# Attention and two MoE layers on one core: 64-column value products, rotated keys in the last score step, and weight units spread over six slots

## Chip, core and metric

The kernel runs on one core of a Trainium2 chip. The metric is the device time of one execution in microseconds. Five engines work side by side, each through its own list of instructions in order: TensorE (PE, with its weight loads listed as PEld), VectorE (DVE), ScalarE (ACT), GpSimd (POOL) and SyncE (SP), which here issues the DMAs.

## What is computed

Attention with a position bias, and then two mixture-of-experts layers of one expert each, over 2304 tokens (4 batches of 576) with 8 heads of 64:

```python
scores = scale * np.matmul(q, k.transpose(0, 1, 3, 2))      # q, k, v: (4, 8, 576, 64)
x = (psi_rel / psi_i)[..., None]                            # from the positions alone
bias = np.maximum(x @ w1 + b1, 0.0) @ w2                    # 32 hidden, 8 heads
scores = scores + bias.transpose(2, 0, 1)[None]
attn = np.exp(scores - np.max(scores, axis=-1, keepdims=True))
attn = attn / (np.sum(attn, axis=-1, keepdims=True) + 1e-09)
x = np.matmul(attn, v)                                      # to (2304, 512)
h = x @ w_in                                                # 512 -> 2048
x = (h * np.clip(h + 3.0, 0.0, 6.0) / 6.0) @ w_out          # 2048 -> 512
gate = 1.0 / (1.0 + np.exp(-(x @ w_gate)))                  # 512 -> 1536
out = (gate * (x @ w_val)) @ w_out2                         # 1536 -> 512
```

## The kernel before

**Stages.** From 0 to 57 us the bias tables are made and written to DRAM (L572 on DVE, L557 on ACT, L578 on PE). From 57 to 341 us stands the attention, and from 341 to 1158 us the two MoE layers.

**Attention.** There are 16 passes (`n`, four pairs of heads by four batches). A pass has nine steps. Steps 0 to 7 take a block of 128 queries of one of the two heads against all 576 keys. Step 8 takes the 64 queries that are left of both heads, the first head's in partitions 0 to 63 and the second's in 64 to 127. One step is: scores on PE (L342, two halves of 288 keys, each from a high and a low part of K), bias added and the minimum taken on DVE (`u`, L346), exponential on ACT (L362), transposes of the probabilities on PE (L400 for 512 of the keys, 128 at a time, evacuated to `ptm` by DVE in L392 or ACT in L390). The 64 keys that are left, the last 64 for the first head and the first 64 for the second, are transposed for both heads in one (L415, `trans_rem`, into `ptr`). In step 8 the two heads lie in the two halves of the partitions of `Pm`, and their 512 keys start at different columns, so there are eight transposes of 64x64 (L408) with two evacuations, and for the rest two transposes (L418, L419) from a tile that has 64 columns of zeros in front.

**Attention times values.** Per half of the queries (`a`), `av` takes four pairs of products with 64 columns of weights, one per head, which go to the two halves of a PSUM bank's partitions (L432), and then one product of 128 weight columns for the rest of the keys of both heads (L435). The matrix unit takes an f32 operand in two passes, so the trace has two records for each such instruction.

**Softmax sums.** `invert` adds 1e-9 to the sums (L368), takes the reciprocal (L369), and ACT spreads them; PE transposes them (L379), and L444 multiplies the product by them.

**Weights for the MoE.** A weight unit is 512 KB. `Loader` takes it in by a DMA on SP (L159) and makes two f32r halves of it: ACT takes the magnitude (L175); DVE does a maximum (L176), a shift (L184) and two merges of raw and shifted words (L186, L188); ACT rounds it (L192) and POOL subtracts (L193). Ten units are prepared during the attention (`NPRE`), each written as one piece (`whole`) every sixth slot (`EVERY`); a slot is two steps. Two more are started by `PRIME` in the last slots.

**What sets the order.** The Tile framework's scheduler puts each instruction into its engine's list by the priority with which the code was written; `tc.issue_after` holds the loader behind the last load of V. In the same stretch POOL makes the low parts of Q and K for the next pass (`prep`, L314 and L318).

## Time and profile before

| | us |
|---|---|
| median of three runs (lowest, highest) | 1158.08 (1157.95, 1161.23) |
| the profiled execution, its span | 1160.52, 1158.7 |
| PE, DVE, ACT, POOL busy | 1135.9, 772.8, 588.4, 422.6 |
| bias tables, 0 to 57: PE, DVE, ACT, POOL busy | 45.51, 50.70, 50.09, 3.32 |
| attention, 57 to 341: the same | 280.78, 222.22, 226.12, 132.22 |
| MoE, 341 to 1158: the same | 809.64, 499.83, 312.20, 287.07 |

The profiled execution is 2.44 us above the median; its granted clock was 0.998 over the span. A busy share is an average over a stage, so the windows have to be read beside it. In a timeline, a row stands for a run of equal instructions; the last one's end is modelled and overlaps the next row, so what a run costs is taken from its start to the start of the next row.

### The profile page before, as it was taken

Reading aid. Unit: us, or ns where it says so; the run is one execution under the profiler, and the core shown is the slowest. Engines: PE = TensorE matmul, PEld = TensorE weight load, DVE = VectorE, ACT = ScalarE, POOL = GpSimd, SP = SyncE. Lnnn points to the kernel's source line nnn. Section 1 sums busy time; section 2 is a strip of 40 time slices with the busy share of each in tenths; the row PEclk is TensorE's granted clock in tenths of the full one; section 3 lists DMA queues with packets and bytes.
Section 4 is the critical chain, followed back from the end, with each engine's and each line's share of the span. In section 5 each row is a group of like instructions: output and inputs, shape, how many; then the busy total and the mean of one; then the engine's idle time right before and its main releaser. Section 6 shows DMA issues by size and latency. Waiting matters only on the chain.

```text
span 1158.7 us, 19146 instructions
## 1 busy us (share of the span) xinstructions
PE 1135.9 (98%) x6862; PEld 1012.2 (87%) x6862; DVE 772.8 (67%) x1495; ACT 588.4 (51%) x1296; POOL 422.6 (36%) x342
## 2 busy tenths in 40 slices
PE   8799999999999999999999999999999999999998
PEld 3277777777779999999999999999899898998997
DVE  8977878788868887355386775585367655644443
ACT  7988887877855545454455454342333222221221
POOL 0154544544316433232347445261333223311211
PEclk9999999999999999999999999999999999999999
DMA  6854436353213665249467759976878848757532
GB/s 203 298 162 110 158 95 183 112 165 103 78 55 110 209 218 200 101 174 340 167 228 255 253 189 357 395 261 251 308 254 309 311 165 299 285 181 258 191 109 73
DMA packets 83183, 236.82 MB, mean 204 GB/s; under 512 B 9616, under 2 KB 12304, under 8 KB 83088
## 3 DMA queue, kind: packets, MB, share of 16 engines
q1 hardware_dynamic: 83088, 235.60, 58.6%
q8 instruction: 54, 0.88, 0.3%
q14 instruction: 41, 0.34, 0.1%
HBM read 154.15 MB, written 81.41 MB: 203 GB/s over the span
## 4 chain that ended last, share of the span: by engine, by line
PE 84%; DVE 6%; ACT 2%; DMA 2%; issue 1%; POOL 1%; SPq 0%; POOLq 0%; DVEq 0%; ACTq 0%
PE o L673 17%; PE h L807 10%; PE o L807 10%; PE s L342 6%; PE o L862 6%; PE h L862 5%; PE h L611 5%; PE h L610 5%; PE h L612 5%; PE av L432 5%; PE tr L400 4%; PE av L435 1%; DVE z L186 1%; DVE u L346 1%; PE tr L379 1%
## 5 line engine op out<-in xcount | busy, mean ns | idle before, releaser
L673 PE MATMUL o<-gh,slot 128*128 128x384 f32 x768 | 196.0, 336 | 1.8 <-DVE take L392 1.8
L673 PEld LDWEIGHTS o<-gh,slot 128*128 128x128 f32 x768 | 139.2, 188 | 2.3 <-DVE take L392 2.1
L673 PE MATMUL o<-gl,slot 128*128 128x384 f32 x384 | 129.1, 336 | 0.7 <-DVE gl L659 0.7
L362 ACT ACTIVATE p<-u,stat 128x576 f32<-128x576 f32 x128 | 98.7, 773 | 29.2 <-DVE stat L346 28.4
L342 PE MATMUL s<-k,q 128*128 128x288 f32 x640 | 111.0, 309 | 0.7 <-ACT ptm L557 0.4
L346 DVE CUSTOM_DVE_ANT_0 u<-s,bias 128x576 f32<-128x576 f32 x128 | 93.6, 753 | 24.4 <-PE s L342 23.2
L843 POOL TENSOR_TENSOR gp<-s,gp 128x384 fp32r<-128x384 f32 x36 | 39.4, 1107 | 177.0 <-ACT gp L842 92.6
L617 DVE SCALAR_TENSOR_TENSOR g<-g,h 128x384 f32<-128x384 f32 x94 | 51.6, 549 | 70.2 <-ACT g L616 70.1
L659 DVE TENSOR_TENSOR gl<-g,gh 128x384 fp32r<-128x384 f32 x94 | 63.1, 671 | 48.3 <-ACT gh L658 45.8
L658 ACT CAST gh<-g 128x384 fp32r<-128x384 f32 x94 | 48.3, 513 | 91.6 <-DVE g L617 91.3
L193 POOL TENSOR_TENSOR hl<-corners,hl 128x512 fp32r<-128x512 f32 x42 | 57.2, 1366 | 94.3 <-ACT hl L192 79.3
L342 PEld LDWEIGHTS s<-k,q 128*128 128x128 f32 x640 | 88.8, 189 | 2.3 <-ACT ptm L557 0.6
L616 ACT ACTIVATE g<-h,half 128x384 f32<-128x384 f32 x94 | 54.3, 578 | 58.4 <-PE h L612 57.9
L807 PE MATMUL o<-x,slot 128*128 128x384 f32 x432 | 78.4, 336 | 1.4 <-DVE sum L787 1.4
L432 PE MATMUL av<-ptm,vn 128*64 128x288 f32 x512 | 77.8, 419 | 0.7 <-DVE x L444 0.7
L807 PE MATMUL h<-x,slot 128*128 128x384 f32 x432 | 77.8, 335 | 0.0
L807 PEld LDWEIGHTS o<-x,slot 128*128 128x128 f32 x432 | 75.1, 188 | 2.0 <-DVE sum L787 1.7
L807 PEld LDWEIGHTS h<-x,slot 128*128 128x128 f32 x432 | 75.2, 188 | 0.7
L400 PE MATMUL tr<-ident,p 128*128 128x128 f32 x512 | 72.2, 275 | 2.2 <-ACT inv L390 1.5
L673 PEld LDWEIGHTS o<-gl,slot 128*128 128x128 f32 x384 | 72.5, 189 | 1.3 <-DVE gl L659 1.3
L314 POOL TENSOR_TENSOR k<-early,one 128x576 fp32r<-128x576 f32 x30 | 34.4, 1167 | 106.3 <-DVE x L572 53.1
L843 POOL TENSOR_TENSOR x<-s,x 128x384 fp32r<-128x384 f32 x36 | 40.3, 1129 | 84.2 <-ACT x L842 50.5
(157 smaller groups left out, 2725.2 us busy)
## 6 DMA issues: line engine op xcount, KB each, us to landing
w<-hl SPq DMA_DIRECT2D x67, 512.0 KB, 3.3
slot<-w SPq DMA_DIRECT2D x67, 512.0 KB, 5.8
raw<-in_part_dram SPq DMA_DIRECT2D x50, 512.0 KB, 4.1
x<-xc SPq DMA_DIRECT2D x56, 384.0 KB, 6.0
sum<-sum SPq DMA_DIRECT2D x72, 256.0 KB, 3.5
early<-xc SPq DMA_DIRECT2D x28, 384.0 KB, 6.4
nbias<-ptm SPq DMA_DIRECT2D x36, 295.5 KB, 3.1
early<-in_part_dram SPq DMA_DIRECT2D x32, 288.0 KB, 4.3
```

The costliest lines, as they stand in the source:

```text
L342: last_s[0] = nc.tensor.matmul(ps[:, a, 0:HS], Q[:, q0 : q0 + P], K[:, r, h, HS * a : HS * a + HS], start=(i == 0), stop=(i == len(mm) - 1))
L346: last_u[0] = nc.vector.tensor_tensor_reduce(out=halves(u), in0=ps[:, :, 0:HS], in1=halves(bt), op0=ALU.add, op1=ALU.min, scale=-0.125, sc ...
L362: nc.scalar.activation(probs(t), us.pop(t), AF.Exp, bias=low[n % 2][:, s : s + 1], scale=-1.0, accum_out=sums[n % 3][:, s : s + 1])
L400: nc.tensor.transpose(ps[:, kc], pts[n, c][:, h, 64 * h + P * kc : 64 * h + P * kc + P], ident)
L432: nc.tensor.matmul(ps[64 * h : 64 * h + 64, 0:HS], vt[:, 4 * h + g], ptm[:, h, g, cols], start=(g == 0), stop=False)
L610: nc.tensor.matmul(ps[:, 0:TW], wh, XH[:, c], start=(c == 0), stop=False)
L611: nc.tensor.matmul(ps[:, 0:TW], wl, XH[:, c], start=False, stop=False)
L659: last_g[0] = nc.vector.tensor_tensor(out=gl, in0=g, in1=gh.bitcast(F32), op=ALU.subtract)
L673: nc.tensor.matmul(os[c][:, 0:TW], sl[:, r, P * c : P * c + P], x, start=(first and r == 0 and x is gh), stop=(last and x is gl))
L807: nc.tensor.matmul(ps[b], sl[:, r, o : o + P], x[:, c, s], start=(k < 4 and i == 0), stop=(i == len(mm) - 1), skip_group_check=True)
L843: nc.gpsimd.tensor_tensor(out=G[:, i, 1], in0=s, in1=G[:, i, 0].bitcast(F32), op=ALU.subtract)
L862: nc.tensor.matmul(os[i], x[:, P * i : P * i + P], slots[(base + 14 + e) % NALL][:, r], start=first, stop=last)
```

## The change

First, `av` takes the last 64 keys as two products of 64 weight columns, one per head, that go to the two halves of the bank as the others do. Second, in step 8 the keys of the second head are taken from the 64th on, and the first 64 at the end, so that both heads' 512 keys lie in the same columns of `Pm`. For this one half of the scores is taken in two parts (224 and 64 keys), the bias of this step is loaded in the same order by one DMA more, and the columns of zeros go. Four transposes of 128x128 with one evacuation (DVE in even passes, ACT in odd) take the place of the eight, and one takes the place of L418 and L419. Third, a weight unit's DMA, magnitude, shift, two merges and last step are written in six slots one after the other, a new unit every 4.5 slots. Fourth, 1e-9 comes from a tile (`tiny`), with a tensor_tensor instead of a tensor_scalar.

```diff
@@ -45,7 +45,6 @@
 
 
 NPRE = 10
-EVERY = 6
 PRIME = (NU * NSTEP // 2 - 2, NU * NSTEP // 2 + 1)
 NALL = 19
 
@@ -108,6 +107,7 @@
     tok = lambda t: [xj[t // 2][:, c, TW * (t % 2) : TW * (t % 2) + TW] for c in range(4)]
     half = keep.tile([P, 1], F32, name="half")
     one = keep.tile([P, 1], F32, name="one")
+    tiny = keep.tile([P, 1], F32, name="tiny")
     slots = [keep.tile([P, 2, 512], F32R, name=f"slot{i}") for i in range(NPRE)]
     nbias = [dram.tile([16 * (8 * RK - 1) * (min(P, S - P * c) // 16) + 16], F32, name=f"nbias{c}") for c in range(5)]
     part_d = [dram.tile([P, 4, TW], F32, name=f"part{t}") for t in range(NTILE)]
@@ -175,18 +175,24 @@
                 nc.scalar.activation(z, raw[..., 1].bitcast(F32), AF.Abs)
                 nc.vector.tensor_scalar(out=z, in0=z, scalar1=2.0**-15, scalar2=None, op0=ALU.max)
 
+        def shift(self, i):
+            z = self.z[i][0].bitcast(I32)
+            nc.vector.tensor_scalar(out=z, in0=z, scalar1=3, scalar2=0x3FFFFFF8, op0=ALU.logical_shift_left,
+                                    op1=ALU.bitwise_and)
+
+        def merge(self, i, w):
+            z, raw = self.z[i]
+            z = z.bitcast(I32)
+            scalar, op = ((29, ALU.logical_shift_right), (-0x40000000, ALU.bitwise_and))[w]
+            nc.vector.scalar_tensor_tensor(out=z, in0=raw[..., w], scalar=scalar, in1=z, op0=op, op1=ALU.bitwise_or)
+
         def assemble(self, i):
             if i not in self.raw:
                 return
             self.raw.pop(i)
-            z, raw = self.z[i]
-            zi = z.bitcast(I32)
-            nc.vector.tensor_scalar(out=zi, in0=zi, scalar1=3, scalar2=0x3FFFFFF8, op0=ALU.logical_shift_left,
-                                    op1=ALU.bitwise_and)
-            nc.vector.scalar_tensor_tensor(out=zi, in0=raw[..., 1], scalar=-0x40000000, in1=zi,
-                                           op0=ALU.bitwise_and, op1=ALU.bitwise_or)
-            nc.vector.scalar_tensor_tensor(out=zi, in0=raw[..., 0], scalar=29, in1=zi,
-                                           op0=ALU.logical_shift_right, op1=ALU.bitwise_or)
+            self.shift(i)
+            self.merge(i, 1)
+            self.merge(i, 0)
 
         def halve(self, z, slot, eng):
             nc.scalar.copy(slot[:, 0], z)
@@ -226,12 +232,19 @@
                 self.mix(to[1], to[2])
             self.done = i + 1
 
-        def whole(self):
-            i = self.n
-            for stage in (self.dma, self.magnitude, self.assemble):
-                stage(i)
-            self.finish(i, nc.gpsimd)
-            self.n += 1
+        def one_step(self, i, k):
+            if k == 0:
+                self.dma(i)
+            elif k == 1:
+                self.magnitude(i)
+                self.raw.pop(i)
+            elif k == 2:
+                self.shift(i)
+            elif k < 5:
+                self.merge(i, 4 - k)
+            else:
+                self.finish(i, nc.gpsimd)
+                self.n = i + 1
 
         def tick(self):
             i = self.n
@@ -275,7 +288,7 @@
     bias_m = apool.tile([P, S], F32, name="bias_m")
     Qs = [apool.tile([P, QW], F32R, name=f"q{i}") for i in range(2)]
     Ks = [apool.tile([P, 2, 2, S], F32R, name=f"k{i}") for i in range(2)]
-    Pm = [apool.tile([P, S + 64], F32, name=f"pm{i}") for i in range(2)]
+    Pm = [apool.tile([P, S], F32, name=f"pm{i}") for i in range(2)]
     ident = apool.tile([P, P], F32, name="ident")
     stat = apool.tile([P, 5, NSTEP], F32, name="stat")
     low, sums = [stat[:, i] for i in range(2)], [stat[:, i] for i in range(2, 5)]
@@ -299,7 +312,12 @@
         rows_of = nbias[c][15 : 15 + n * (8 * RK - 1)].rearrange("(i q) -> i q", i=n)
         for h in range(2):
             o = bias_t[c][:, h] if c < 4 else bias_m[64 * h : 64 * h + 64]
-            nc.sync.dma_start(o, rows_of[:, RK * (2 * p + h) : RK * (2 * p + h) + S])
+            i = rows_of[:, RK * (2 * p + h) : RK * (2 * p + h) + S]
+            if c == 4 and h == 1:
+                nc.sync.dma_start(o[:, 0:512], i[:, 64:S])
+                nc.sync.dma_start(o[:, 512:S], i[:, 0:64])
+            else:
+                nc.sync.dma_start(o, i)
 
     def prep(n, h, on=PREP_ON):
 
@@ -330,17 +348,23 @@
 
     seq = [(n, s) for n in range(NU) for s in range(NSTEP)]
 
+    def keys(s, h, a):
+
+        if s < 8 or h == 0:
+            return [(HS * a, 0, HS)]
+        return [(64, 0, HS)] if a == 0 else [(64 + HS, 0, HS - 64), (0, HS - 64, 64)]
+
     def scores(t):
         n, s = seq[t]
         Q, K = Qs[n % 2], Ks[n % 2]
         ps = pp.tile([P, 2, 512], F32, name="s")
         todo = [(s % 2, s // 2)] if s < 8 else [(0, 4), (1, 4)]
         for a in range(2):
-            mm = [(h, c, r) for h, c in todo for r in range(2)]
-            for i, (h, c, r) in enumerate(mm):
+            mm = [(h, c, r, part) for h, c in todo for r in range(2) for part in keys(s, h, a)]
+            for i, (h, c, r, (k0, o, w)) in enumerate(mm):
                 q0 = (0, S + P)[h] + P * c if c < 4 else (512, S)[h]
-                last_s[0] = nc.tensor.matmul(ps[:, a, 0:HS], Q[:, q0 : q0 + P], K[:, r, h, HS * a : HS * a + HS],
-                                 start=(i == 0), stop=(i == len(mm) - 1))
+                last_s[0] = nc.tensor.matmul(ps[:, a, o : o + w], Q[:, q0 : q0 + P], K[:, r, h, k0 : k0 + w],
+                                             start=(i == 0), stop=(i == len(mm) - 1))
         u = a2.tile([P, S], F32, name="u", bufs=3)
         bt = bias_t[s // 2][:, s % 2] if s < 8 else bias_m
         last_u[0] = nc.vector.tensor_tensor_reduce(
@@ -355,7 +379,7 @@
             if h == 0:
                 pts[n, c] = a2.tile([P, 2, S], F32, name="p", bufs=3)
             return pts[n, c][:, h]
-        return Pm[n % 2][:, 64:]
+        return Pm[n % 2]
 
     def expo(t):
         n, s = seq[t]
@@ -365,7 +389,7 @@
     def invert(n, c0, c1):
 
         r = sums[n % 3][:, 2 * c0 : min(2 * c1, NSTEP)]
-        nc.vector.tensor_scalar(out=r, in0=r, scalar1=1e-9, scalar2=None, op0=ALU.add)
+        nc.vector.tensor_tensor(out=r, in0=r, in1=tiny.to_broadcast(r.shape), op=ALU.add)
         nc.vector.reciprocal(r, r)
         for s0, s1, w in ((0, 6, 64),) if c1 == 3 else ((6, 8, 64), (8, 9, P)):
             o = spread[:, 64 * s0 : 64 * s0 + (s1 - s0) * w].rearrange("p (s w) -> p s w", w=w)
@@ -400,25 +424,19 @@
                 nc.tensor.transpose(ps[:, kc], pts[n, c][:, h, 64 * h + P * kc : 64 * h + P * kc + P], ident)
             evac(PT_EVAC[s], ptm[:, h, :, P * c : P * c + P], ps)
         else:
-            pm = Pm[n % 2]
-            for h in range(2):
-                ps = pp.tile([P, 4, P], F32, name="tr", bufs=3)
-                r = slice(64 * h, 64 * h + 64)
-                for kc in range(4):
-                    nc.tensor.transpose(ps[:, kc, 0:64], pm[r, 64 + 64 * h + P * kc : 64 + 64 * h + P * kc + P],
-                                        ident[r, r])
-                evac("AV"[h], ptm[:, h, :, 512:S], ps[:, :, 0:64])
+            ps = pp.tile([P, 4, P], F32, name="tr", bufs=3)
+            for kc in range(4):
+                nc.tensor.transpose(ps[:, kc], Pm[n % 2][:, P * kc : P * kc + P], ident)
+            evac("VA"[n % 2], ptm[:, :, :, 512:S], ps.rearrange("p c (h q) -> p h c q", h=2))
 
     def trans_rem(n, c):
 
         ps = pp.tile([P, 4, P], F32, name="tr", bufs=3)
         nc.tensor.transpose(ps[:, 0], pts[n, c].rearrange("p h s -> p (h s)")[:, 512 : 512 + P], ident)
         if c == 3:
-            pm = Pm[n % 2]
-            nc.tensor.transpose(ps[:, 1], pm[:, 0:P], ident)
-            nc.tensor.transpose(ps[0:64, 2], pm[:, S : S + 64], ident)
-            evac("A", ptr[0:64, 512:S], ps[0:64, 2, 0:64])
-            evac("V", ptr[64:P, 512:S], ps[64:P, 1, 64:P])
+            nc.tensor.transpose(ps[0:64, 1], Pm[n % 2][:, 512:S], ident)
+            for h in range(2):
+                evac("AV"[h], ptr[64 * h : 64 * h + 64, 512:S], ps[0:64, 1, 64 * h : 64 * h + 64])
         evac("A", ptr[:, P * c : P * c + P], ps[:, 0])
 
     def av(n, a, g):
@@ -432,7 +450,8 @@
                 nc.tensor.matmul(ps[64 * h : 64 * h + 64, 0:HS], vt[:, 4 * h + g], ptm[:, h, g, cols],
                                  start=(g == 0), stop=False)
         else:
-            nc.tensor.matmul(ps[:, 0:HS], vt[:, 8:10].rearrange("p a d -> p (a d)"), ptr[:, cols], start=False, stop=True)
+            for h in range(2):
+                nc.tensor.matmul(ps[64 * h : 64 * h + 64, 0:HS], vt[:, 8 + h], ptr[:, cols], start=False, stop=True)
 
     def av_out(n, a):
         p, b = divmod(n, B)
@@ -516,6 +535,7 @@
         nc.vector.memset(warm, 0.0)
         nc.vector.memset(half, 0.5)
         nc.vector.memset(one, 1.0)
+        nc.vector.memset(tiny, 1e-9)
         nc.scalar.activation(low[0][:, 0:1], one, AF.Relu)
         bias_ps = ExitStack()
         bp = bias_ps.enter_context(tc.tile_pool(name="bp", bufs=4, space=PSUM))
@@ -524,8 +544,6 @@
             nc.tensor.matmul(ps, warm[:, 0:P], warm, start=True, stop=True)
         load_qk(0)
         make_identity(nc, ident)
-        for i in range(2):
-            nc.gpsimd.memset(Pm[i][:, 0:64], 0.0)
 
         nc.vector.tensor_scalar(out=tbl, in0=tbl, scalar1=w1c, scalar2=None, op0=ALU.mult)
         nc.vector.tensor_scalar(out=bpsi[:, 0], in0=psi, scalar1=b1c[:, 0:1], scalar2=None, op0=ALU.mult)
@@ -630,9 +648,11 @@
             if i in (NS // 2 + 1, NS // 2 + 2):
                 f = len(begun)
                 begun[f] = hardswish(ring("z")[:, 0:TW], project(0, slots[2 * f], pp.tile([P, 2, 512], F32, name="s")[:, 0]))
-            if i % EVERY == 0 and i > 10 and load.n < NPRE:
-                with tc.issue_after(last_v[0].ins):
-                    load.whole()
+            for m in range(NPRE):
+                at = i - NSTEP * (m + 1) // 2
+                if 0 <= at <= 5:
+                    with tc.issue_after(last_v[0].ins):
+                        load.one_step(m, at)
             if i in PRIME:
                 load.tick()
 
```

PE, step 8 of the second pass, with its transposes between the scores of the pass after it. Before:

```order
L400 MATMUL tr<-ident,p 128x128 x4
L408 MATMUL tr<-ident,pm_233 128x64 x4
L342 MATMUL s<-k_230,q_228 128x288 x4
L408 MATMUL tr<-ident,pm_233 128x64 x4
L342 MATMUL s<-k_230,q_228 128x288
L415 MATMUL tr<-ident,p 128x128
L418 MATMUL tr<-ident,pm_233 128x128
L419 MATMUL tr<-ident,pm_233 64x128
L342 MATMUL s<-k_230,q_228 128x288 x3
L432 MATMUL av<-ptm,vn 64x288 x2
L435 MATMUL av<-ptr,vn 128x288
```

and now:

```order
L424 MATMUL tr<-ident,p 128x128 x4
L429 MATMUL tr<-ident,pm_234 128x128 x4
L366 MATMUL s<-k_231,q_229 128x288 x5
L435 MATMUL tr<-ident,p 128x128
L437 MATMUL tr<-ident,pm_234 64x128
L366 MATMUL s<-k_231,q_229 128x288 x3
L450 MATMUL av<-ptm,vn 64x288 x2
L454 MATMUL av<-ptr,vn 64x288 x2
```

The two blocks of four small transposes have become one block of four, one of the three single transposes is gone, and the last product has become two.

DVE, where the attention begins: L572 (now L590) is the last operation of the bias tables, and L346 (now L370) the first `u`. Before:

```order
L572 TENSOR_SCALAR x_64<-x_65,early 128x576 x2
L572 TENSOR_SCALAR x_65<-x_65,early 128x576 x2
L346 ISA u,stat<-s,bias_223 128x576
L346 ISA stat 128x1
L346 ISA u,stat<-s,bias_223 128x576
```

and now:

```order
L590 TENSOR_SCALAR x_64<-x_65,early 128x576 x2
L590 TENSOR_SCALAR x_65<-x_65,early 128x576 x2
L176 TENSOR_SCALAR z<-z 128x512
L180 TENSOR_SCALAR z<-z 128x512
L187 SCALAR_TENSOR_TENSOR z<-raw,z 128x512 x2
L370 ISA u,stat<-s,bias_224 128x576
L370 ISA stat 128x1
```

All four DVE operations of the first weight unit stand ahead of the first `u`. Its DMA is now the tenth on SP's list and its magnitude stands early on ACT's, both among the bias tables.

DVE, the second weight unit, in the second pass. Before, this place has no weight unit:

```order
L346 ISA u,stat<-s,bias_223 128x576
L346 ISA stat 128x1
L368 TENSOR_SCALAR stat<-stat 128x3
L369 RECIPROCAL stat<-stat 128x3
L346 ISA u,stat<-s,bias_224 128x576
L346 ISA stat 128x1
```

and now:

```order
L370 ISA u,stat<-s,bias_224 128x576
L370 ISA stat 128x1
L392 TENSOR_TENSOR stat<-stat,tiny 128x3
L176 TENSOR_SCALAR z<-z 128x512
L393 RECIPROCAL stat<-stat 128x3
L180 TENSOR_SCALAR z<-z 128x512
L187 SCALAR_TENSOR_TENSOR z<-raw,z 128x512 x2
L370 ISA u,stat<-s,bias_225 128x576
L370 ISA stat 128x1
```

The four operations of a weight unit stand between the sums of a pass and the next `u`. The sixth and the tenth unit stand in the same way; of the others, work of the attention lies between the operations. From the last steps of the attention on, the lists of all engines are in the order of before.

## Rows read from the trace of the kernel before

**Rows 1.** Part 1 of the page: busy us (share of span) x instructions.
```profile
PE 1135.9 (98%) x6862; PEld 1012.2 (87%) x6862; DVE 772.8 (67%) x1495; ACT 588.4 (51%) x1296; POOL 422.6 (36%) x342
```

**Rows 2.** Windows; busy us (instructions) of PE, PEld, DVE, ACT, POOL; clock, DMA.
```profile
125.00:155.00 30.00, 29.09 (x215) 22.42 (x216) 26.31 (x64) 23.36 (x60) 14.00 (x11) 1.00 0.36 108
195.00:225.00 30.00, 29.05 (x216) 22.52 (x216) 26.67 (x62) 23.36 (x63) 14.42 (x12) 1.00 0.36 104
265.00:295.00 30.00, 29.06 (x216) 22.53 (x217) 26.69 (x63) 23.36 (x60) 14.77 (x12) 1.00 0.38 115
```

**Rows 3.** Timeline of PE, second attention products: start us, us, instruction, count.
```profile
109.76 1.68 PE L432 MATMUL av<-ptm,vn 128*64 128x288 f32 x12
111.37 0.44 PE L379 MATMUL tr<-ident,spread 128*128 128x128 f32 x2
...
113.90 0.71 PE L432 MATMUL av<-ptm,vn 128*64 128x288 f32 x4
114.54 0.75 PE L435 MATMUL av<-ptr,vn 128*128 128x288 f32 x2
115.13 0.60 PE L400 MATMUL tr<-ident,p 128*128 128x128 f32 x4
```

**Rows 4.** Timeline of PE, one step-8 transpose block cut in two.
```profile
121.81 0.60 PE L400 MATMUL tr<-ident,p 128*128 128x128 f32 x4
122.34 0.46 PE L408 MATMUL tr<-ident,pm 64*128 64x64 f32 x4
...
123.46 0.46 PE L408 MATMUL tr<-ident,pm 64*128 64x64 f32 x4
123.85 0.40 PE L342 MATMUL s<-k,q 128*128 128x288 f32 x1
```

**Rows 5.** Timeline of PE, a step-8 transpose block in one piece.
```profile
141.12 0.75 PE L435 MATMUL av<-ptr,vn 128*128 128x288 f32 x2
141.80 0.47 PE L408 MATMUL tr<-ident,pm 64*128 64x64 f32 x8
142.21 0.33 PE L415 MATMUL tr<-ident,p 128*128 128x128 f32 x1
```

**Rows 6.** Timeline of PE, plain scores and plain transposes.
```profile
116.03 1.83 PE L342 MATMUL s<-k,q 128*128 128x288 f32 x12
117.70 0.60 PE L400 MATMUL tr<-ident,p 128*128 128x128 f32 x4
118.13 0.27 PE L415 MATMUL tr<-ident,p 128*128 128x128 f32 x1
```

**Rows 7.** Timeline of POOL and DVE, a merge in the middle of attention.
```profile
126.39 1.41 POOL L318 TENSOR_TENSOR q<-early,q 64x576 fp32r<-64x576 f32 x1 [2.22 <-ACT q L310]
126.44 1.92 DVE L186 SCALAR_TENSOR_TENSOR z<-raw,z 128x512 int32<-128x512 int32 x1
```

**Rows 8.** Timeline of DVE, a merge with POOL idle.
```profile
339.67 0.69 DVE L188 SCALAR_TENSOR_TENSOR z<-raw,z 128x512 int32<-128x512 int32 x1
```

**Rows 9.** Durations of L368 in ns: min/median/max, first and last start.
```profile
L368 DVE TENSOR_SCALAR stat<-stat x32: 160/168/1149, 65.9 to 328.7; 128x6 f32<-128x6 f32 x16, 128x3 f32<-128x3 f32 x16
```

**Rows 10.** Timeline of POOL where attention begins; in brackets the idle before.
```profile
54.55 2.86 POOL L314 TENSOR_TENSOR k<-early,one 128x576 fp32r<-128x576 f32 x2 [53.12 <-DVE x L572]
57.49 1.55 POOL L318 TENSOR_TENSOR q<-early,q 64x640 fp32r<-64x640 f32 x1
59.12 2.82 POOL L318 TENSOR_TENSOR k<-early,k 128x576 fp32r<-128x576 f32 x2
```

**Rows 11.** Timeline of DVE, the same place.
```profile
57.76 0.76 DVE L346 CUSTOM_DVE_ANT_0 u<-s,bias 128x576 f32<-128x576 f32 x1 [2.46 <-PE s L342]
...
60.88 0.69 DVE L392 COPY ptm<-tr 128x512 f32<-128x512 f32 x1
62.02 0.76 DVE L346 CUSTOM_DVE_ANT_0 u<-s,bias 128x576 f32<-128x576 f32 x1 [0.46 <-ACT p L362]
```

**Rows 12.** The chain of waits, the same place: start us, us, what.
```profile
58.24 3.62 DMA bias<-nbias
```

## Prediction

> **What bounds the kernel now.** I read the page's first part first: PE is busy for 98% of the span [rows 1], so an edit pays where it takes time from PE, and costs where PE has to wait longer. The change moves nothing behind the last steps of the attention, so I then took the attention in windows, to see where PE is not full. In three stretches of 30 us, where weight units are prepared, PE is busy for 29.09, 29.05 and 29.06 us [rows 2]: .91, .95 and .94 us of stalls, 2.8 in all. Elsewhere in the attention PE has no gap to speak of. In such a stretch DVE is busy for 26.31 us and idle for 3.7 [rows 2]; it is the second engine and has little to spare. Last I took PE's timeline and priced each kind of instruction from the start of its run to the start of the next row, since the ends are modelled.
>
> **The products of attention and values.** There are 32 halves (16 passes, two each). Twelve records of L432 take 111.37 − 109.76 = 1.61 us, and four take 114.54 − 113.90 = .64 [rows 3]. Eight more records cost .97, so one is .121 and what is left over for a run is .15. The 128-column product, L435, takes 115.13 − 114.54 = .59 [rows 3]. Before, the last products are .64 + .59 = 1.23; after, eight records in one run are .97 + .15 = 1.12. That is .11 per half, and 32 × .11 = **3.5 us less**. All of it lies on PE. That the two new products run side by side, like those of L432, is assumed from their having the same shape and the same two halves of the bank.
>
> **The transposes of step 8.** In 7 passes the eight small ones stand in two blocks of four. From the L400 ahead of them to the score behind them 123.85 − 121.81 = 2.04 us pass [rows 4]. In it lie four L400, 118.13 − 117.70 = .43, and four scores of .139 (twelve take 117.70 − 116.03 = 1.67), .56 [rows 6], so 1.05 is left for the eight. They become four of the plain kind, .43, and of the three single ones one goes, .11 (a quarter of .43). 1.05 + .11 − .43 = .73, times 7 = 5.1 us. In the other 9 passes the eight stand in one block: 142.21 − 141.80 = .41 [rows 5], no more than four plain ones (.43). What is gained is one single transpose, .11, and the change of shape: from L435 to the block takes .68 [rows 5] where L435 has .59 [rows 3], so .09. .41 − .43 + .11 + .09 = .18, times 9 = 1.6 us. Together **6.7 us less**. One evacuation of 512 columns on DVE or ACT takes the place of two of 256; neither engine is the bound there, and I cost it at nothing. If this cover were gone it would be worth a few tenths per pass at most, in the stretches with stalls, which stand below.
>
> **The scores in two parts.** Per pass two products of 288 keys become four of 224 and 64, so 32 products are added and no column. If a small product starts as soon after the last as the 64x64 transposes do, .051 (.41 for 8, [rows 5]), it costs .051 less its share of columns (64/288 of .139 = .031), .02 each, 0.7 us in all. If it takes as long as a plain transpose, which has 128 columns of weights as it has, .108 [rows 6], it costs .077 each, 2.5 us. Below nothing it can't go, since instructions are added and no work is taken away. I take **0.7 more**, by the row with the same 64 columns, and keep 2.5 for the range. The Trainium skill ("TensorE: Matmul & The Clock Gate", section "LDWEIGHTS (loading the stationary operand)") gives a weight load about its columns divided by 1.2 in ns, 107 for 128 columns, whatever follows; by that the two parts would take at least 214 ns where one product takes 139, and the term would be an estimated 2.4 us. The rows of plain transposes fit that; no row here has a small product with 128 columns of weights in this type.
>
> **The entry of the attention.** All four DVE operations of the first weight unit now stand ahead of the first u. There DVE has 2.46 us of idle time before 57.76 [rows 11]. Alone the four would take about .43 + .43 + .69 + .69 = 2.24 (the merge: .69 with POOL idle [rows 8]; the two others are estimated at four tenths, the same size with one input) and would just fit. But POOL works back to back from 54.55 to 62 [rows 10], and a merge under a POOL operation waits: 1.92 us instead of .69, with the POOL operation of 1.41 that began .05 us earlier [rows 7, 8]. If only the two merges wait, the first until 57.41, and the second behind the next POOL operation of 1.55, u starts at about 60.35; if all four take turns with POOL, at about 62.5. u is so 2.6 to 4.7 late. Not all of it counts: the fifth u waits for a bias DMA that ends at 61.86 and starts at 62.02 [rows 11, 12]. The four u and the copy ahead of it take 3.6 us of work (57.76 to 61.57, less .2 of gaps [rows 11]), so it starts at 63.95 to 66.1, 1.9 to 4.1 late. I take **3.0 more**. PE has nothing else in its list to fill this time, since the scores of the next steps wait for banks that u reads. The end below is nothing, if the four fit into the idle time after all.
>
> **The weight units in the attention.** The number of operations is the same; what changes is what stands beside them. The second, sixth and tenth unit have the four operations in one piece between the sums and u, where each can meet a POOL operation; I give them the loss of a stretch of before, .93 each, 2.8 in all, as before. In the six others the operations stand apart with u and evacuations between them; the stretch of before had its merges between u as well, so I give each .07, **0.4 more** together, with 2.8 less (all stalls gone) and 3 more for the ends. Queued behind a waiting merge on DVE are the u of the next step, and behind that ACT's exponential and PE's transposes.
>
> **1e-9 by a tensor operand.** L368 takes .168 us at the median and up to 1.149 [rows 9], so it too waits at times, about a POOL operation long. If the new form did not wait, DVE would get back up to one us in some passes, which pays only where DVE stalls PE, inside the 2.8 above. I cost it at nothing. The Trainium skill ("SBUF — State Buffer", section "Who interferes with whom") speaks against this edit: a DVE instruction with two SBUF inputs contends with a GpSimd instruction that reads SBUF, and a tensor_tensor is named as such; by it the new form would wait as the old did, and the sum stays. That a merge with two SBUF inputs waits [rows 7] agrees; no row has the new form.
>
> The removed columns of zeros and the extra DMA (one more issue on SP in each of four pairs) have nobody waiting for them.
>
> **The sum.** −3.5 − 6.7 + 0.7 + 3.0 + 0.4 = −6.1. The profiled execution would go from 1160.52 to 1154.4; it lies 2.44 above the median of 1158.08, so for the median I say **1152.0 us**. A difference under 0.3%, 3.5 us, can't be told from no change; the bounds of that are 1154.6 and 1161.6.
>
> **Rivals.**
>
> 1. *The entry is free.* The four operations fit into the 2.46 us, either because the first run before POOL is deep in its list, or because the order of waiting turns out kinder. For it: 2.24 is under 2.46. Against it: POOL has no gap from 54.55 to 62 [rows 10], and merges do wait [rows 7]. It gives 1152.0 − 3.0 = 1149.0, and 1146 if the spreading also takes the stalls away.
>
> 2. *The small products cost a plain row.* Splitting the scores costs 2.5 instead of 0.7, and the entry its upper end, 4.1: 1152.0 + 1.8 + 1.1 = 1154.9, which is within 0.3%. For it: a plain transpose with 128 columns of weights starts .108 after the last [rows 6]. Against it: those of 64 columns start .051 apart [rows 5].
>
> 3. *Slower: DVE becomes the bound in passes with a weight unit.* If each of the four operations waits for a whole POOL operation (1.41 [rows 7]), a unit costs DVE 5.6 us of waiting. One merge's wait, 1.2, is in the trace now. DVE's idle time is 3.7 of 30 us [rows 2], 2.1 for a pass of 17.4 (30 us hold 1.7 passes), so 5.6 − 1.2 − 2.1 = 2.3 would come out of PE for each of nine units, 21 us, against the gain of 9.5 on PE that is left without the entry; with the entry at 3.0 it comes to 1158.1 − 9.5 + 3.0 + 21 = 1172. It decides from about 1.1 us per unit on: there the gain is eaten. Against it: POOL is busy for only 14.00 of 30 us [rows 2], and six of nine units are spread, so that few meet four POOL operations.
>
> 4. *The change does not do what it says:* the two new products don't run side by side. Then eight records are four of L432 and four single ones of at least .121, .48 more than the 1.12, and 32 × .48 = 15 us would turn the sum into 1167. L432's own rows speak against it, as the pairs there have the same shape.
>
> **How the numbers follow.** The forecast, 1149.5 to 1154.6, has 0.48. The first rival has 0.24 (1145.5 to 1149.5), the second 0.18 (1154.6 to 1158), the third 0.06, the fourth 0.02, and 0.02 are left for a gain beyond 1145.5. The range 1145.5 to 1156.5 leaves out the slower cases and the upper end of the second rival. Faster by over 0.3% holds the forecast, the first rival and the rest below: 0.74. Within 0.3% are the second rival and the mild half of the third, which ends near 1158: 0.20. Slower is 0.06.
>
> **What the profile after would show.** Right: eight records of L450 and L454 in about 1.12 us; four L429 in .43, with the scores behind them unbroken; the first u near 61 us, with the operations of the weight unit ahead of it stretched to 1.4 us and more; some stalls left at the second, sixth and tenth unit. Wrong: a first u before 59 (rival 1), parts of 64 keys .1 or more apart (rival 2), DVE without idle time in most passes and PE waiting for u in each (rival 3).

## The result and the profile after

The changed kernel takes 1171.68 us (median of 4 runs, 1170.96 to 1172.11), and the kernel before beside it 1158.53: a ratio of 1.0108 with an interval of 1.0091 to 1.0126, slower by 13.2 us. The forecast was 1152.0, in a range of 1145.5 to 1156.5. The profiled execution has a span of 1170.3 us, 11.6 more than before.

Part 1 of the page of the changed kernel [rows 1]:

```profile
PE 1138.5 (97%) x6878; PEld 1014.6 (87%) x6878; DVE 783.2 (67%) x1488; ACT 586.8 (50%) x1288; POOL 426.7 (36%) x340
```

DVE has seven instructions fewer and is busy 10.4 us longer: they got slower, not more. By the starts of u in both traces, the attention's last u is 10.8 us late. Most of this delay is added at four places, within a few microseconds each. The windows of the changed kernel at these four show them (columns as in [rows 2]):

```profile
58.00:68.00 10.00, 6.99 (x44) 6.74 (x44) 8.20 (x17) 6.50 (x15) 7.71 (x6) 0.83 0.86 252
92.00:104.00 12.00, 9.57 (x58) 6.27 (x57) 8.98 (x20) 7.75 (x22) 4.73 (x4) 0.86 0.29 75
164.00:176.00 12.00, 9.79 (x62) 7.31 (x62) 9.86 (x19) 8.16 (x22) 5.86 (x4) 0.86 0.29 75
234.00:246.00 12.00, 10.49 (x71) 6.86 (x71) 11.49 (x25) 9.92 (x27) 7.51 (x6) 1.00 0.52 151
```

PE is without work for 1.5 to 3.0 us in each, and in the first three the granted clock is 0.83 to 0.86 on top. These are the places of the first, second, sixth and tenth weight unit, the ones whose four DVE operations stand in one piece. The second unit in DVE's timeline:

```profile
90.13 0.29 DVE L392 TENSOR_TENSOR stat<-stat,tiny 128x3 f32<-128x3 f32 x1
90.34 0.41 DVE L176 TENSOR_SCALAR z<-z 128x512 f32<-128x512 f32 x1
90.68 0.16 DVE L393 RECIPROCAL stat<-stat 128x3 f32<-128x3 f32 x1
90.79 1.52 DVE L180 TENSOR_SCALAR z<-z 128x512 int32<-128x512 int32 x1
92.35 3.74 DVE L187 SCALAR_TENSOR_TENSOR z<-raw,z 128x512 int32<-128x512 int32 x2
96.01 0.74 DVE L370 CUSTOM_DVE_ANT_0 u<-s,bias 128x576 f32<-128x576 f32 x1
```

and POOL's at the same time:

```profile
90.48 1.55 POOL L336 TENSOR_TENSOR k<-early,k 128x576 fp32r<-128x576 f32 x1
92.11 3.43 POOL L336 TENSOR_TENSOR q<-early,q 64x640 fp32r<-64x640 f32 x2
```

The shift takes 1.52 us, and the two merges 3.74, where a merge alone takes .69 [rows 8]. DVE and POOL take turns, operation by operation, and the u behind them starts 5.2 us after the shift, where the three operations alone would take 1.8. PE's timeline shows it standing before the scores, and again before the transposes of the step:

```profile
96.82 0.67 PE L366 MATMUL s<-k,q 128*128 128x288 f32 x3 [0.87 <-DVE stat L370]
98.62 0.33 PE L424 MATMUL tr<-ident,p 128*128 128x128 f32 x1 [1.14 <-ACT ptr L414]
```

Right behind this the granted clock of TensorE (the third column from the end, as a share of 2.4 GHz) falls:

```profile
92.00:98.00 6.00, 4.20 (x29) 2.69 (x27) 5.87 (x10) 3.40 (x11) 3.46 (x3) 1.00 0.57 147
98.00:104.00 6.00, 5.38 (x29) 3.57 (x30) 3.11 (x12) 4.35 (x12) 1.27 (x1) 0.72 0.02 3
```

PE was idle for 1.8 of 6 us at full clock, and then runs at a mean of 0.72 of 2.4 GHz, which is about 3.4 us at the lower level of 1.2 GHz. If PE's time goes with its clock there, that costs an estimated 6 x .28 = 1.7 us more. By the times of u this place costs 3.8 us in all, the sixth unit's the same and the tenth's, where the clock stays at 1.00, 3.2.

At the entry of the attention the first u starts at 60.56, 2.8 later than in [rows 11], and PE waits for it. DVE's timeline, and PE's row:

```profile
55.34 0.41 DVE L176 TENSOR_SCALAR z<-z 128x512 f32<-128x512 f32 x1
55.78 1.25 DVE L180 TENSOR_SCALAR z<-z 128x512 int32<-128x512 int32 x1
57.07 3.46 DVE L187 SCALAR_TENSOR_TENSOR z<-raw,z 128x512 int32<-128x512 int32 x2
60.56 0.76 DVE L370 CUSTOM_DVE_ANT_0 u<-s,bias 128x576 f32<-128x576 f32 x1
```

```profile
61.38 1.85 PE L366 MATMUL s<-k,q 128*128 128x288 f32 x7 [3.01 <-DVE stat L370]
```

And there is something in the MoE, which the change doesn't touch. The groups of the changed kernel, busy us and mean ns, and behind them the same groups of the kernel before:

```profile
L827 PE MATMUL o<-x,slot 128*128 128x384 f32 x432 | 79.4, 340 | 0.0
L827 PE MATMUL h<-x,slot 128*128 128x384 f32 x432 | 79.3, 340 | 0.0
L882 PE MATMUL h<-slot,x 128*128 128x512 f32 x162 | 40.8, 396 | 0.4 <-ACT x L862 0.4
```

```profile
L807 PE MATMUL o<-x,slot 128*128 128x384 f32 x432 | 78.4, 336 | 1.4 <-DVE sum L787 1.4
L807 PE MATMUL h<-x,slot 128*128 128x384 f32 x432 | 77.8, 335 | 0.0
L862 PE MATMUL h<-slot,x 128*128 128x512 f32 x162 | 40.1, 392 | 0.4 <-ACT x L842 0.4
```

The 864 products with 384 columns of the operand `x` take 4 to 5 ns more each at the mean. So do, by 2 to 4 ns, the four groups of 162 products in which `slot` has the 512 columns; one of them is shown. The other products with 384 columns stay at 334 to 336 ns.

### The profile page after: what moved, and what is told of

It is laid out like the page before. It is cut to its first block, busy times and chain, and to the rows that moved or that the text cites. A ratio compares the mean times of both kernels' runs of the same rounds, so it can differ in the third digit from the quotient of the medians.

```text
span 1170.3 us, 19205 instructions
## 1 busy us (share of the span) xinstructions
PE 1138.5 (97%) x6878; PEld 1014.6 (87%) x6878; DVE 783.2 (67%) x1488; ACT 586.8 (50%) x1288; POOL 426.7 (36%) x340
## 4 chain that ended last, share of the span: by engine, by line
PE 80%; DVE 8%; ACT 5%; issue 2%; POOL 1%; DMA 1%; DVEq 0%; ACTq 0%; POOLq 0%; SPq 0%
PE o L693 16%; PE h L827 11%; PE o L827 10%; PE o L882 6%; PE h L882 6%; PE h L630 5%; PE h L628 5%; PE h L629 5%; PE s L366 4%; PE av L450 4%; PE tr L424 4%; DVE u L370 2%; ACT p L386 2%; DVE z L187 1%; PE av L454 1%
## 5 line engine op out<-in xcount | busy, mean ns | idle before, releaser
L366 PE MATMUL s<-k,q 128*128 128x288 f32 (+2 forms) x672 | 112.9, 308 | 5.7 <-DVE stat L370 5.3
L370 DVE CUSTOM_DVE_ANT_0 u<-s,bias 128x576 f32<-128x576 f32 x128 | 93.6, 753 | 20.9 <-PE s L366 18.2
L366 PEld LDWEIGHTS s<-k,q 128*128 128x128 f32 x672 | 93.9, 193 | 6.7 <-DVE stat L370 6.0
L187 DVE SCALAR_TENSOR_TENSOR z<-raw,z 128x512 int32<-128x512 int32 x76 | 79.9, 1053 | 1.0
L424 PE MATMUL tr<-ident,p 128*128 128x128 f32 x512 | 75.3, 281 | 4.3 <-ACT ptr L414 3.0
```

Of the source, the lines that this page charges most:

```text
L187: nc.vector.scalar_tensor_tensor(out=z, in0=raw[..., w], scalar=scalar, in1=z, op0=op, op1=ALU.bitwise_or)
L366: last_s[0] = nc.tensor.matmul(ps[:, a, o : o + w], Q[:, q0 : q0 + P], K[:, r, h, k0 : k0 + w], start=(i == 0), stop=(i == len(mm) - 1))
L370: last_u[0] = nc.vector.tensor_tensor_reduce(out=halves(u), in0=ps[:, :, 0:HS], in1=halves(bt), op0=ALU.add, op1=ALU.min, scale=-0.125, sc ...
L424: nc.tensor.transpose(ps[:, kc], pts[n, c][:, h, 64 * h + P * kc : 64 * h + P * kc + P], ident)
```

## The parts one by one

The theory at this point: DVE operations in one piece under POOL operations, and the place of the new tile, make the loss, and the gain on PE is there. The rival: the gain on PE is not there, or one of the two PE edits loses by itself. Four kernels make one part of the change each, on one chip (kernel before there: 1158.50). The later runs stand on other chips, on which the kernel before takes 1158.66 to 1159.13, so a difference between kernels on two chips can be off by some .6 us.

**Products alone.**

```diff
-            nc.tensor.matmul(ps[:, 0:HS], vt[:, 8:10].rearrange("p a d -> p (a d)"), ptr[:, cols], start=False, stop=True)
+            for h in range(2):
+                nc.tensor.matmul(ps[64 * h : 64 * h + 64, 0:HS], vt[:, 8 + h], ptr[:, cols], start=False, stop=True)
```

> Before with only the two 64-column products in place of L435. If the term of 3.5 us stands on PE, where it was priced, the time falls by 3 to 4 us against before. The rival, that the gain is lost in waits of the attention, gives a difference under 1 us.

1158.56 us, ratio 0.9998 (0.9989 to 1.0007): no difference that can be told, and at most 1.3 us of gain. In its trace the eight records do take 1.12 us in place of 1.23, and 1.12 in place of 1.33 ahead of a block of step 8. But of each gain of .10 to .11, .05 to .07 is gone at the next run of transposes, and as much again soon after it. The last u is only some 1.3 us earlier than in the kernel with the tile alone (below), whose attention is that of before but for the new form. So most of the gain is lost in the attention itself; that PE came early to work that was not ready is the likely reason, and not shown place by place.

**Rotated keys alone.**

```diff
-    Pm = [apool.tile([P, S + 64], F32, name=f"pm{i}") for i in range(2)]
+    Pm = [apool.tile([P, S], F32, name=f"pm{i}") for i in range(2)]
...
+                nc.tensor.transpose(ps[:, kc], Pm[n % 2][:, P * kc : P * kc + P], ident)
+            evac("VA"[n % 2], ptm[:, :, :, 512:S], ps.rearrange("p c (h q) -> p h c q", h=2))
```

> Before with only the rotated keys of step 8 (transposes, split scores, bias in two DMAs). The trace after shows runs of 14 scores at 1.94 us before a product, where 12 had 1.77, so the split costs about .05 to .09 for each of 32, 1.6 to 2.8 us, and the transposes give some 6 back: the time falls by 3 to 5 us. The rival, that the new step 8 is the reason of the loss, makes it slower by 5 us and more.

1164.79 us, 1.0048 (1.0034 to 1.0062), slower by 6.3: the rival's side, though not by its mechanism. The operations of three units now stand in one piece, with the loader's code untouched. In every second pass DVE has one evacuation less; that this is why the scheduler moved them is not shown. DVE's timeline of this kernel at the first of them:

```profile
121.10 0.94 DVE L176 TENSOR_SCALAR z<-z 128x512 f32<-128x512 f32 x1 [0.81 <-ACT z L175]
121.96 0.16 DVE L380 RECIPROCAL stat<-stat 128x3 f32<-128x3 f32 x1
122.08 1.65 DVE L184 TENSOR_SCALAR z<-z 128x512 int32<-128x512 int32 x1
123.76 1.79 DVE L186 SCALAR_TENSOR_TENSOR z<-raw,z 128x512 int32<-128x512 int32 x1
125.59 0.69 DVE L188 SCALAR_TENSOR_TENSOR z<-raw,z 128x512 int32<-128x512 int32 x1
```

At these three places ACT also waits .7 to 1.4 us for the unit's DMA before the magnitude. Each costs 2.3 to 2.7 us by the length of its pass.

**Spreading alone.**

```diff
+                at = i - NSTEP * (m + 1) // 2
+                if 0 <= at <= 5:
+                    with tc.issue_after(last_v[0].ins):
+                        load.one_step(m, at)
```

> Before with only the weight units spread over six slots. If the DVE operations in a row under POOL operations are the cause of the loss, with the half clock behind each long wait of PE, this kernel is slower than before by 12 to 18 us, more than the changed one. If the loss comes from the other edits, it is within 3 us of before.

1163.46 us, 1.0037 (1.0023 to 1.0051), slower by 5.0, of which 3.8 in the attention, 3.1 of them at its entry. The theory wanted 12 to 18: refuted as it stood. In this company only the first unit, at the entry, is in one piece. At the second, sixth and tenth unit the spreading brings that about only together with the rotated keys.

**The tile alone.**

```diff
+    tiny = keep.tile([P, 1], F32, name="tiny")
...
-        nc.vector.tensor_scalar(out=r, in0=r, scalar1=1e-9, scalar2=None, op0=ALU.add)
+        nc.vector.tensor_tensor(out=r, in0=r, in1=tiny.to_broadcast(r.shape), op=ALU.add)
```

> Before with only 1e-9 from a tile by a tensor_tensor. In the trace after, the 864 products of L827 with the operand x take 340 ns at the median, before 335, and nothing else in the MoE does: 864 x 5 ns = 4.3 us. If the place of the tiles in memory does that, through the one new tile in the pool that stays, this kernel is slower by 4 us in the MoE layers. If it is the order or the loader, it is within 1 us of before.

1162.83 us, 1.0033 (1.0021 to 1.0046), slower by 4.3 as expected. The x products take 340 ns in its trace too. That "nothing else in the MoE does" was wrong, though: the products with 512 columns of `slot` are slower here as well (394 to 396 ns for 391 to 392).

Moving the tile in the changed kernel from the pool that stays to the one that is given back takes the place apart from the operation.

```diff
-    tiny = keep.tile([P, 1], F32, name="tiny")
+    tiny = apool.tile([P, 1], F32, name="tiny")
```

> The changed kernel with the new tile moved from the pool that stays to the attention's pool, which is given back before the MoE. If its place shifts what stands behind it, and that alone makes the x products 5 ns longer each, they go back to 335 ns and the time falls by 4 to 5 us, to about 1167. If not, it stays at 1171 to 1172.

1168.15 us: 3.5 less than the changed kernel, and the products are back, those of `slot` at 391 to 392 ns too:

```profile
L827 PE MATMUL o<-x,slot 128*128 128x384 f32 x432 | 78.0, 335 | 0.0
L827 PE MATMUL h<-x,slot 128*128 128x384 f32 x432 | 77.8, 335 | 0.0
```

So it is the place of the tile, with the same operation. Against this kernel the two groups of x are busy 2.9 us longer in the changed one and the four of `slot` 1.8, 4.7 together; 864 x 5 ns came to 4.3 in part by chance, as the products overlap and four groups were left out. By the kernel's text the slots are allocated behind the new tile in the same pool. Which address makes the difference was not tried.

The change without the spreading:

> The changed kernel with the weight units written in one piece every sixth slot, as before. If the parts add up (products 0, rotated keys 6.3, tile 4.3 us alone), it is at 1168 to 1170, and the spreading costs 2 to 4 us in this company. If the spreading is what makes the rotated keys slow, it falls to 1161 or less.

1166.65 us, 8.0 over before where the three parts alone add up to 10.6. The spreading costs 5.0 in this company as it does alone. Here the pieces stand where the rotated keys alone put them, so the spreading moves them to other places and adds the entry.

## Is it POOL?

> The changed kernel without POOL's part of the preparation of Q and K from the third pass on (high part of K, low parts of both; the scores then use old ones). The order of every DVE instruction is the same as in the changed kernel, so the pieces of four stay. If they cost because each waits for a POOL operation, the steps at the second (3.8), sixth (3.9) and tenth unit (3.2 us) all but the second go, as its POOL work belongs to the third pass they all go, and the time falls by 9 to 12 us to 1160 to 1163, with the entry left. If the pieces cost because of their own length on DVE, it stays within 3 us.

```diff
         high(on[0], Q[0:D], qt)
-        high(on[1], K[:, 0], kt)
-        low(on[2], Q[D:P], qt, Q[0:D])
-        low(on[3], K[:, 1], kt, K[:, 0])
+        if n < 2:
+            high(on[1], K[:, 0], kt)
+            low(on[2], Q[D:P], qt, Q[0:D])
+            low(on[3], K[:, 1], kt, K[:, 0])
```

1161.27 us, 10.4 less. DVE's list is the same, instruction by instruction. The second unit in this kernel:

```profile
90.81 0.43 DVE L176 TENSOR_SCALAR z<-z 128x512 f32<-128x512 f32 x1
91.16 0.17 DVE L394 RECIPROCAL stat<-stat 128x3 f32<-128x3 f32 x1
91.27 0.43 DVE L180 TENSOR_SCALAR z<-z 128x512 int32<-128x512 int32 x1
91.74 1.42 DVE L187 SCALAR_TENSOR_TENSOR z<-raw,z 128x512 int32<-128x512 int32 x2
93.17 0.76 DVE L371 CUSTOM_DVE_ANT_0 u<-s,bias 128x576 f32<-128x576 f32 x1
```

The shift takes .43 for 1.52 and the merges 1.42 for 3.74, and the delays at the second, sixth and tenth unit are gone from the times of u. In the attention of the changed kernel neither PE nor DVE waits for a result of POOL, and ACT does once, for 1.4 us, so what the quiet POOL gives back is the meeting with DVE and not the lateness of POOL's own results. The same edit in the kernel before:

> The kernel before without POOL's part of the preparation of Q and K from the third pass on. If the three stalled stretches of before, 2.8 us, come from merges under POOL operations, the time falls by 2 to 3 us, to about 1156; the changed kernel lost 10.4 us in the same way, so the change would have added some 8 us of this kind. If it stays at 1158 to 1159, the stalls of before were no collisions, and all of the 10.4 is new.

1157.09 us beside 1158.66, so 1.6 less, a little under the 2 to 3. Of the 10.4 us, 8.8 are then new collisions. But this kernel's DVE list is not quite that of before: the second unit's first operations stand 2.5 us later in their pass, and PE stands once before a bank there, 1.1 us, which it does not in the kernel before:

```profile
PE tr L401 <- ACT ptr L391: 1.1, 1, 1.1
```

By the times of u this kernel gains 1.3 to 1.4 us at each of the two later stretches of [rows 2] and nothing at this one. In the order of before it would have gained an estimated 1.3 more, so 8.8 is an upper figure and 7.5 the lower one.

The prediction's entry term was tried by itself, with only the first unit held behind the last u of its slot (`last_u` for `last_v`, for `m == 0`).

> The changed kernel with only its first weight unit held behind the last u of its slot; the others as changed. The order then has no weight unit ahead of the first u, and the second unit comes apart as well (its four operations have attention work between them). By the times of u the entry costs 3.4 and the second unit 3.8 us, so the time falls by 6 to 8 us, to 1164 to 1166. If the delay at the entry is caught up later, it falls by 4 us at most.

1164.58 us, 7.1 less than the changed kernel, as expected. The first u starts at 57.59. By the times of u the two kernels are 3.8 us apart ahead of the second unit, 6.4 behind it, 8.2 behind the sixth, where the clock stays at 2.4 GHz here, and 7.4 at the end: the entry reaches the end, and of the second unit's 3.8 some 2.6 do.

## Can the units be spread without the loss?

All units held behind the last u of their slot:

```diff
-                    with tc.issue_after(last_v[0].ins):
+                    with tc.issue_after(last_u[0].ins):
                         load.one_step(m, at)
```

> The changed kernel with the weight units' steps held behind the last u of their slot instead of the last load of V. In the order the four DVE operations of a unit then have 7 to 10 instructions of the attention between each two, nothing stands ahead of the first u, and the second, sixth and tenth unit are no longer in one piece. If the pieces cause the loss (entry 3.4, and 3.8, 3.9 and 3.2 us at three places by the times of u), the time falls by 10 to 14 us, to 1158 to 1161. If operations that stand apart meet POOL just as often and cost as much, it stays within 3 us of 1171.7.

> The same, and without the new tile: 1e-9 is added as before. It should be 4 to 5 us below the one before it, 1154 to 1156.5, and so a little under the kernel before, if the gain of the products and the transposes is not eaten elsewhere; 1158 to 1160 if it is.

1170.72 us, and 1165.38 without the tile. Nothing is in one piece any more, nothing stands at the entry, and yet the first is only 1.0 under the changed kernel. This looked like the end of the theory. ACT's timeline of the second of them shows a new wait:

```profile
121.54 0.68 ACT L174 ACTIVATE z<-raw 128x512 f32<-128x512 f32 x1 [2.68 <-DMA raw<-in_part_dram]
```

In every second pass ACT stands up to 2.7 us before a magnitude whose DMA has not landed, and the exponentials are queued behind it; the view of waits of ACT sums it:

```profile
ACT z L174 <- DMA raw<-in_part_dram: 11.4, 6, 2.7
```

With the DMA behind the last load of V, as in the changed kernel, and the rest behind the last u, and the same without the rotated keys:

> The kernel with products, rotated keys and the units held behind the last u, without the new tile (1165.4 so far), but with a unit's DMA held behind the last load of V as in the changed kernel. In 1165.4 ACT stands 2.4 to 2.7 us before the magnitude in every second pass, since the unit's DMA has not landed. In the new order the magnitude stands 14 to 17 instructions later on ACT. If that wait is what the spread units still cost, it goes at four places and the time falls by 8 to 10 us, to 1155 to 1158. If the cost is the collision of spread operations with POOL, it stays at 1163 to 1166.

> The same without the rotated keys. Alone the rotated keys cost 6.3 us, by putting the four DVE operations of three units in one piece. With the units held behind the last u that can't happen; then the rotated keys should be a gain of 2 to 4 us, and this kernel slower by that than the one before it. If the rotated keys cost through their own waits (one evacuation of 512 columns on one engine), this kernel is the faster one, by 3 us and more.

1161.67 us (three of its nine runs near 1159.6, six near 1162) and 1166.60. The wait of ACT is gone from the attention, for 3.7 us, not 8 to 10. And the rotated keys, which cost 6.3 alone, are worth 4.9 here. What is left over before is 3 us. The same kernel with a quiet POOL:

> The kernel with products, rotated keys and units held behind the last u with an early DMA (1161.7), here without POOL's part of the preparation of Q and K from the third pass on, as in the two quiet kernels (1157.1 for before, 1161.3 for the changed one). If the gain of 9.5 us that the prediction gave to PE is there and only collisions hide it, this is 1147 to 1149. If PE waits for evacuations in its place even without collisions, as the passes without a weight unit suggest (0.12 to 0.15 us a pass), it is 1153 to 1156.

1152.19 us. DVE's list is the same as in the kernel of 1161.67, so in this order too, with nothing in one piece, meeting POOL costs 9.5 us. And it is 4.9 below the quiet kernel before (1157.09). So with nothing to collide, products and rotated keys bring 4.9 us at most and not 9.5; without the quiet kernel before's own odd place it would be an estimated 3.6. The forecast's 1147 to 1149 is refuted, and 1152.2 lies just under the other theory's range.

POOL is idle in a part of each pass. The units' DVE operations moved into it:

```diff
-                at = i - NSTEP * (m + 1) // 2
-                if 0 <= at <= 5:
-                    with tc.issue_after(last_v[0].ins):
-                        load.one_step(m, at)
+                for st in {0: (0,), 2: (1,), 3: (2, 3), 4: (4, 5)}.get(i - NSTEP * (m + 1) // 2, ()):
+                    with tc.issue_after((last_v[0] if st == 0 else last_u[0]).ins):
+                        load.one_step(m, st)
```

> The same kernel with POOL at work, and the magnitude, shift and merges moved two slots later and closer together, into the part of a pass in which POOL is idle (some 9 to 15 us after the pass's first u). If collisions are what is left of the cost, it falls from 1161.7 to 1155 to 1157, below before. If the length of DVE's own work is the cost, it stays at 1160 to 1163.

> The same with the four DVE operations two slots later, one to a slot, so that half of them still meet POOL. By collisions it lies between the kernel before this one in the list and 1161.7, at 1158 to 1160.

1153.47 us (ratio 0.9959, 0.9946 to 0.9971) and 1160.96. The first has the same operations as the kernel of 1161.67. By its edit the magnitude and the shift are one slot later, not two, the merges in the slots where they were, and the last step one earlier; in the trace the shift stands 13 us behind the first u of its pass, in place of 8.5 to 10, with the first merge .5 to 1.5 us behind it, in place of some 4. It nearly reaches the quiet kernel, and it is 5.2 us faster than the kernel before. The second has all four two slots later, one to a slot, and its .7 less can't be told from no gain. In the trace of the first, with its DVE and POOL rows from 180 us on, the shift and the merges of one unit take what they take alone, and POOL starts behind the shift and the first merge. The next unit's last merge still meets POOL (203.62), as that of every second unit does:

```profile
182.03 0.42 DVE L179 TENSOR_SCALAR z<-z 128x512 int32<-128x512 int32 x1
182.49 0.69 DVE L186 SCALAR_TENSOR_TENSOR z<-raw,z 128x512 int32<-128x512 int32 x1
...
185.11 0.69 DVE L186 SCALAR_TENSOR_TENSOR z<-raw,z 128x512 int32<-128x512 int32 x1
...
203.62 1.39 DVE L186 SCALAR_TENSOR_TENSOR z<-raw,z 128x512 int32<-128x512 int32 x1
```

```profile
183.95 1.15 POOL L331 TENSOR_TENSOR k<-early,one 128x576 fp32r<-128x576 f32 x1 [6.00 <-PE s L365]
```

One place with operations of two units among each other was left, at the end of the loader's work. It takes `PRIME`'s ticks behind the last u as well:

> The kernel with the units' operations in POOL's idle part (1153.5), with the eleventh and twelfth unit, which are started at the end of the attention, held behind the last u as well. In the kernel of 1153.5 the eleventh unit's operations stand right among those of the tenth, and u loses 3 us there. If that is the same kind of loss, this is 1150 to 1152; but the eleventh unit is then prepared after the attention, where DVE and the MoE's first tile may pay for it, and the time stays at 1153 to 1154.

1152.88 us, 0.9941 (0.9928 to 0.9955), beside the kernel before at 1159.13 on that chip. Its gain over the one with `PRIME` as it was, .6 us, can't be told from none; its last u of the attention stands 1.7 us earlier. It is the best version found, 6 us under the kernel before.

## Why the prediction was wrong, step by step

**The weight units** are the step that failed: "0.4 more". It put the three units in one piece at .93 each, the loss of a stretch of before, though it said that each of their operations can meet a POOL operation. They cost 3.8, 3.8 and 3.2, and new collisions come to 7.5 to 8.8 us in all. In a stretch of before one merge waits 1.23 us for POOL [rows 7, 8], and the next unit's maximum and shift 1.3 together, with other work between them. In one piece three of the four wait at the second and sixth unit, 3.4 us together, and two at the tenth, 2.5; u waits behind them, and at the first two the clock falls as well. The prediction had said of the first unit that "all four take turns with POOL" and priced that; it did not give the same to the second, the sixth and the tenth, of which it knew that they stand in the same way.

**The third rival** had this mechanism and ended at 1172. The time came out right for a wrong sum: it gave 2.3 us to each of nine units, 21 in all, where the runs show 8.8 at most, most of it at three units; what filled most of the gap was the tile (4.3) and the gain that was not there (4.6 at least). That was luck.

**The tile** was costed at nothing, by the DVE operation alone. The operation costs nothing, as told: the durations of the new form in the changed kernel are

```profile
L392 DVE TENSOR_TENSOR stat<-stat,tiny x32: 154/164/1166, 69.4 to 339.4; 128x6 f32<-128x6 f32 x16, 128x3 f32<-128x3 f32 x16
```

against 160/168/1149 [rows 9]. It waits as the old did, which is what the Trainium skill's rule ("SBUF — State Buffer", section "Who interferes with whom") made of it, and the trace agrees. What was not priced is the place of the new tile: in the pool that stays it costs 4.3 us in the MoE, in a stage that the prediction left out because its order is unchanged. That it does so by shifting the tiles behind it is the likely way; no address was read.

**The products and the transposes** were priced right at their place. Eight records take 1.12 us as forecast (204.77 to 205.89 here), and a block of step 8 .36 ahead of scores and .44 to .50, as here, ahead of a single transpose, where .43 was forecast:

```profile
204.77 0.71 PE L450 MATMUL av<-ptm,vn 128*64 128x288 f32 x4
205.30 0.66 PE L454 MATMUL av<-ptr,vn 128*64 128x288 f32 x4
205.89 0.44 PE L403 MATMUL tr<-ident,spread 128*128 128x128 f32 x2
...
214.26 2.01 PE L366 MATMUL s<-k,q 128*128 128x288 f32 x14
216.20 1.68 PE L450 MATMUL av<-ptm,vn 128*64 128x288 f32 x12
...
221.34 0.66 PE L429 MATMUL tr<-ident,pm 128*128 128x128 f32 x4
221.84 0.27 PE L435 MATMUL tr<-ident,p 128*128 128x128 f32 x1
```

"All of it lies on PE" is so, but that it therefore reaches the end was the mistake: 4.9 of the 9.5 at most do, with nothing colliding. Three pieces of the rest are seen. The single transposes behind (now L435) wait for a bank that ACT still evacuates, 1.1 us in the quiet kernel; the quiet kernel before has none ahead of these, and the one of 1.1 shown above elsewhere. The changed kernel's group:

```profile
L435 PE MATMUL tr<-ident,p 128*128 128x128 f32 x63 | 18.2, 288 | 2.7 <-ACT inv L414 2.6
```

The runs of transposes ahead of a single one take .05 longer in some 20 more places than in the quiet kernel before, 1 us. And the **scores in two parts** were mis-sized: 14 of them take 216.20 − 214.26 = 1.94, where 12 ahead of a product took 1.77 before, and ahead of a transpose 1.77 for 1.67. .17 for two at 8 places and .10 at 8 make 2.2 us, not 0.7, and close to the bound of 2.5. The 2.4 by the Trainium skill ("TensorE: Matmul & The Clock Gate", section "LDWEIGHTS (loading the stationary operand)") was nearer than the row that I took, and the trace agrees: from 215.14 to 215.58 the weight loads of the split products, 128 columns each, start .11 us apart, so a pair of parts takes .22 and not .139. Of the 4.6 at least 1 us is not traced, and more if the gain is the lower 3.6.

**The entry** was right: 3.0 forecast, 2.8 at the first u, 3.4 by the times of u some steps later, within the range of 1.9 to 4.1. Three of the four operations wait there. The size has some luck in it, as the lower clock behind the wait (0.83 from 58 to 68), which the prediction did not have, is in the 3.4.

The sum: −6.1 forecast, +13.2 measured, 19.3 apart. The tile 4.3, collisions 8.8 in place of 0.4, the gain on PE 4.9 in place of 9.5, the entry .4 more: 4.3 + 8.4 + 4.6 + .4 = 17.7. The odd place of the quiet kernel before moves 1.3 us from the collisions to the missing gain and leaves the sum. The parts are not exactly additive and each is known to a microsecond or so, and 1.6 stays open.

## To carry to other kernels

Work that fills gaps on a second engine has to be placed against the engine that it blocks, and not only spread: the same operations, spread, cost 9.5 us by meeting POOL, and 8.2 of these went when the shift stood 3 to 4 us later in the pass and the merges close behind it. An edit elsewhere in the list can let the scheduler move others together, so read the order of every engine for pieces of such work, and price each piece by turns with the blocker, not by the average of before. And a stage whose instructions don't change can still change its time, if a new tile lives on beside its operands: put small new tiles where they are given back, or look at the products' mean duration first.

## What the hardware showed that was not expected

One new tile of a single f32 column in a lasting pool made 864 products with one operand take 340 ns in place of 335, and 648 with another 393 to 396 in place of 391 to 392, with the rest unchanged; moving the tile to a pool that is given back undid it. A DVE operation with a single input (the shift, 128x512) waits for POOL as long as one with two does: 1.52 us for .43. TensorE's granted clock fell behind PE's waits at three places: after 1.8 us of waits in the 6 ahead of 98 and 1.3 in the 6 ahead of 170 its mean was 0.72 for the next 6, and after 3.0 at the entry it was 0.83 from 58 to 68. At the tenth unit, with 1.5 us of waits in 12, it stayed at 2.4 GHz, and so it did all through the attention of the kernel without the spreading, which has three such pieces. What makes the difference is not shown.
